# One row a lane of a projection weight loaded by GpSimd in four transfers, in a decode attention block

## The chip, the cores and the metric

The kernel runs on one core of a Trainium2 chip. The metric is device time in microseconds (us). A core has a matrix engine (PE), a vector engine (DVE), a scalar engine (ACT), GpSimd (POOL) and a sync engine (SP) that here only issues transfers. Sixteen DMA engines move data between the device memory and the on-chip memory, which has 128 lanes.

## The reference

One decode step of two blocks side by side on the same normalised input, added to it. `A` is attention with a cached K and V, `B` a gated MLP.

```python
x = A_x                                    # (4, 1, 640)
xn = _layernorm(x, axis=-1)
# A: 32 heads of 128, K and V caches of 4 x 32 x 4096 x 128, all bfloat16
q = (xn @ wq).reshape(B, Sq, Hq, Dh).transpose(0, 2, 1, 3)
scores = jnp.einsum('bhqd,bhkd->bhqk', q, k) * Dh ** (-0.5)
o = jnp.einsum('bhqk,bhkd->bhqd', _softmax(scores), v)
a = o.transpose(0, 2, 1, 3).reshape(B, Sq, Hq * Dh) @ wo      # wo: 4096 x 640
# B: w_in 640 x 1728, w_out 864 x 640
z = gelu(xn @ w_in); z1 = z[..., :864]; z2 = _layernorm(z[..., 864:])
g = einsum('ts,bsf->btf', w_sp, z2) + b_sp
return x + a + (z1 * g) @ w_out
```

Nearly all bytes are the two caches: 2 x 134 MB. The weights add 5.2 (wq), 5.2 (wo), 2.2 (w_in) and 1.1 MB (w_out).

## The kernel before, in words

The work is cut into 16 runs `i`, each one batch row and eight heads. A run's K is 128 lanes by 64 KB, as is its V. A large tile `ring` of 11 units (16 KB a lane each) holds whatever is in flight: wq first, then K of a run in four units, V in four, the weights of `B` for a while, and at the end `wo`.

**Loads.** Every large load is issued by SP, in the order of the list `loads` (lines 195 to 211): K of run 0 in halves, `w_in` and `w_out`, K and V in turn, and `load_wos` last. `pump()` (line 216) is called as units are given back and issues the next loads whose place is free, so SP is generally a transfer or two ahead of what is being moved. The last 96 rows of `w_out` come in six short transfers (`load_edge`, line 146), each 16 lanes of 1,280 B seen as 4 x 4.

**The projection weight.** `wo` is seen as four blocks `j` of 128 lanes by eight rows by 640 columns (line 168): a lane has eight rows of 1,280 B in a block, 10,240 B in one piece. `load_wo(j)` (line 172) loads blocks 0 to 2 by one transfer each and block 3 by three, cut at rows 5 and 7 (`WO_CUTS`). All six go out late, through `load_wos`, when the last V has its place.

**Compute.** For each quarter of K, DVE multiplies by q (`product`, line 542) and folds the halves (`fold`, line 551); PE adds up through an identity matrix (line 560), DVE finishes the row sums (line 573); then come the maximum, the exponential on ACT, and on PE the sums over V (`blocks`, line 635). At the end `group_proj` (line 747) multiplies each of the four head groups with its block of `wo`: eight rows `hh` by four column parts, 32 matmuls a block, in the order of the blocks. `res` is copied out of PSUM by ACT and DVE (lines 839 and 840), and SP and ACT store it.

**Order.** The lists of PE, DVE, ACT and SP inside `manual_schedule` are written out by hand. GpSimd's own list is short: some memsets, the identity, 16 small casts into `place` (line 294) that wait for `lane_diag` from DVE, and four small products late (line 695). A framework orders the instructions outside `manual_schedule` on each engine and inserts the waits. Near the start, `x` is normalised, transposed, and multiplied by wq (line 346); `stage_q` (line 516) spreads q over the lanes with `place`, and the result `qbc` is what `product` reads.

Of the kernel before, what the change touches and what calls it, by code (L numbers as in the profile page):

```python
# [10 lines left out]
BF16 = mybir.dt.bfloat16  # L11
# [9 lines left out]
def kernel(  # L21
# [14 lines left out]
    nc = tc.nc  # L36
    P = nc.NUM_PARTITIONS
    Bsz, Sq, D = A_x.shape
# [9 lines left out]
    HT = 8  # L48
# [24 lines left out]
    NOQ = D // CG  # L73
# [7 lines left out]
    const = ctx.enter_context(tc.tile_pool(name="const", bufs=1))  # L81
# [11 lines left out]
    def units(first, n=1):  # L93
        return ring[:, first * UNIT : (first + n) * UNIT]
# [73 lines left out]
    wo_r = A_wo.rearrange("(j p r) n -> j p (r n)", p=P, r=HT)  # L168
    wo_tiles = {}
    WO_CUTS = (0, 5 * D, 7 * D, HT * D)  # L170

    def load_wo(j):
        t = units(WO_UNIT, UNITS - WO_UNIT)[:, j * HT * D : (j + 1) * HT * D]
        wo_tiles[j] = t.rearrange("p (r n) -> p r n", r=HT)
        cuts = (0, HT * D) if j < HG - 1 else WO_CUTS
        for c0, c1 in zip(cuts, cuts[1:]):
            nc.sync.dma_start(out=t[:, c0:c1], in_=wo_r[j][:, c0:c1])

    def load_wos():
        for j in range(HG):  # L180
            load_wo(j)
# [34 lines left out]
    def pump():  # L216
        while loads:
# [21 lines left out]
        out=lane_diag[:],  # L239
        in_=ident_f[:].rearrange("p (h l) -> p l h", h=HT),  # L240
# [5 lines left out]
        out=hmask[:],  # L246
        in_=ident_f[:].rearrange("p (h l) -> p h l", h=HT),
# [5 lines left out]
        out=head_scale[:].rearrange("p (h l) -> p h l", h=HT),  # L253
# [11 lines left out]
        out=sel[:],  # L265
        in_=ident_f[:].rearrange("p (g h k) -> p k h g", g=CG, k=GC),
# [5 lines left out]
        out=spread[:],  # L272
        in_=ident[:].rearrange("p (m r) -> p r m", r=HT)[:, :, None, :].to_broadcast(
            [P, HT, HT, LN]
        ),
# [3 lines left out]
        out=q_lanes[:].rearrange("r b (h l) -> r b h l", h=HT),  # L279
        in_=ident[: HT * Bsz, : HT * Bsz]  # L280
# [9 lines left out]
    for g in range(CG):  # L290
        ps = slice(g * QW, (g + 1) * QW)
        for hh in range(QH):
            at_col = (g % 2 * QH + hh) * Bsz
            nc.gpsimd.tensor_copy(
                out=place[ps, hh, at_col : at_col + Bsz], in_=lane_diag[ps, 0:Bsz]
            )

    hmask_bf = const.tile([P, HT], BF16)
    nc.vector.tensor_copy(out=hmask_bf[:], in_=hmask[:])
# [8 lines left out]
    for i in range(NSTAT):  # L308
# [5 lines left out]
        out=rstd[:], in_=mv[:, 1:2], func=ACT.Sqrt, bias=eps_tile[:Bsz], scale=1.0  # L314
# [4 lines left out]
        out=xn_bf[:],  # L319
# [9 lines left out]
    for c in range(DC):  # L329
        nc.tensor.transpose(  # L330
            out=xnT_ps[:, c, :], in_=xn_v[:, c, :], identity=ident[:Bsz, :Bsz]
# [11 lines left out]
    for c in range(DC):  # L343
        for hg in range(NQG):
            g = hg % CG
            nc.tensor.matmul(
                out=q_ps[hg // CG][g * QW : (g + 1) * QW, :],
                lhsT=xnT[:, c, :],
                rhs=wq_sb[:, c, hg * QH * Dh : (hg + 1) * QH * Dh],
# [9 lines left out]
    def out_sum(half):  # L359
        return out_ps[OG * half : OG * half + Bsz, :]  # L360

    for half in range(2):
        nc.tensor.matmul(
            out=out_sum(half),
            lhsT=ident[:Bsz, :Bsz],
            rhs=x_bf[:, half * NOH : (half + 1) * NOH],
# [299 lines left out]
    def out_last(part):  # L666
        half, c = divmod(part, 2)
        at = OG * (2 * c + half)
        return finals[c][at : at + Bsz, 0:NOQ]
# [77 lines left out]
    def group_proj(hg):  # L747
        for hh in range(HT):
            for part in range(CG):
                nc.tensor.matmul(  # L750
                    out=out_last(part),
                    lhsT=gr[hg][:, hh, :],
                    rhs=wo_tiles[hg][:, hh, part * NOQ : (part + 1) * NOQ],
                    start=False,
                    stop=(hg == HG - 1 and hh == HT - 1),
                )

    E = mybir.EngineType
    with tc.manual_schedule(engines={E.PE, E.DVE, E.Activation, E.SP}):
# [73 lines left out]
        for hg in range(HG):  # L833
            group_proj(hg)
# [38 lines left out]
```

## Time and profile before

| | |
|---|---|
| median of 3 runs | 661.55 us (661.41 to 661.88) |
| the profiled execution | 661.42 us, span 659.3 us |
| bytes read | 282.24 MB, 428 GB/s over the span |
| DVE busy | 492.7 us (75%) |
| PE busy | 316.0 us (48%), granted clock 0.67 |
| ACT busy | 86.1 us (13%) |
| POOL busy | 8.5 us (1%), 31 instructions |

The profiled execution is one run with its own time; the span lies between its first and last instruction. In the views, a group of instructions stands under its line in the kernel, its engine and `tile written<-tile read`. The chain of waits goes back from the last instruction through whatever released it. A landing is the moment at which a DMA engine reports that its part of a transfer has arrived.

### The profile page before, as it was taken

Reading aid. Unit: us, or ns where it says so; the run is one execution under the profiler, and the core shown is the slowest. Engines: PE = TensorE matmul, PEld = TensorE weight load, DVE = VectorE, ACT = ScalarE, POOL = GpSimd, SP = SyncE. Lnnn points to the kernel's source line nnn. Section 1 sums busy time; section 2 is a strip of 40 time slices with the busy share of each in tenths; the row PEclk is TensorE's granted clock in tenths of the full one; section 3 lists DMA queues with packets and bytes.
Section 4 is the critical chain, followed back from the end, with each engine's and each line's share of the span. In section 5 each row is a group of like instructions: output and inputs, shape, how many; then the busy total and the mean of one; then the engine's idle time right before and its main releaser. Section 6 shows DMA issues by size and latency. Waiting matters only on the chain.

```text
span 659.3 us, 4830 instructions
## 1 busy us (share of the span) xinstructions
PE 316.0 (48%) x2063; PEld 144.2 (22%) x2063; DVE 492.7 (75%) x286; ACT 86.1 (13%) x208; POOL 8.5 (1%) x31
## 2 busy tenths in 40 slices
PE   0257552807446272644627165362715537245855
PEld 0114220302213130221303022130312213112323
DVE  2497968959496795949779494986949498699830
ACT  0023110020202002020210202002020200202000
POOL 3000000000000000000000000000000000000000
PEclk9676685755868566586856658685666868556776
DMA  9999999999999999999999999999999999999997
GB/s 380 433 449 418 432 441 437 426 446 437 422 437 418 441 442 425 441 430 421 441 445 430 441 418 430 441 434 433 438 421 437 431 429 438 445 425 422 426 429 301
DMA packets 6649, 282.56 MB, mean 429 GB/s; under 512 B 760, under 2 KB 996, under 8 KB 1380
## 3 DMA queue, kind: packets, MB, share of 16 engines
q1 hardware_dynamic: 6608, 282.24, 99.1%
q8 instruction: 16, 0.26, 0.1%
q14 instruction: 5, 0.04, 0.0%
q10 hardware_dynamic: 20, 0.01, 0.0%
HBM read 282.24 MB, written 0.01 MB: 428 GB/s over the span
## 4 chain that ended last, share of the span: by engine, by line
DMA 68%; DVE 21%; PE 10%; issue 1%; ACT 0%; SPq 0%; DVEq 0%
DMA ring<-in_A_k_cache_dram 60%; DVE ring L542 13%; PE s_ps L560 9%; DVE ring L551 7%; DMA ring<-in_A_wo_dram 4%; DMA ring<-in_A_v_cache_dram 4%; PE zT L405 1%; DVE s_sb L573 0%; PE s_ps L750 0%; PE max_ps L586 0%; PE ac_ps L483 0%; DVE m L582 0%; SPq L112 0%; DVE res L840 0%; ACT lay L584 0%
## 5 line engine op out<-in xcount | busy, mean ns | idle before, releaser
L542 DVE TENSOR_TENSOR ring<-ring,qbc 128x8192 bf16<-128x8192 bf16 x64 | 282.7, 4417 | 78.5 <-DMA ring<-in_A_k_cache_dram 78.5
L560 PE MATMUL s_ps<-ring,ident 128*128 128x512 bf16 x512 | 188.7, 535 | 248.0 <-DVE ring L551 248.0
L551 DVE TENSOR_TENSOR ring<-ring 128x4096 bf16<-128x4096 bf16 x64 | 146.6, 2291 | 2.0
L560 PEld LDWEIGHTS <-ident 128*128 128x128 bf16 x512 | 64.3, 129 | 356.3 <-issue 259.2
L635 PE MATMUL pv_acc<-ring,pm 128*32 128x512 bf16 x1024 | 83.7, 482 | 31.4 <-DMA ring<-in_A_v_cache_dram 31.4
L573 DVE TENSOR_REDUCE s_sb<-s_ps 128x64 f32<-128x512 f32 x64 | 43.8, 684 | 29.9 <-PE s_ps L560 29.9
L635 PEld LDWEIGHTS <-pm 128*32 128x32 bf16 x1024 | 44.6, 148 | 66.3 <-issue 57.9
L648 ACT COPY pv_sb<-pv_acc 128x512 f32<-128x512 f32 x16 | 9.4, 586 | 327.8 <-PE pv_acc L635 327.8
L607 ACT ACTIVATE pm<-p,hmask 128x256 bf16<-128x256 bf16 x120 | 49.5, 494 | 0.5
L652 PE MATMUL pv<-sel,pv_sb 128*128 128x8 f32 x128 | 16.9, 259 | 11.2 <-ACT pv_sb L648 11.2
L586 PE MATMUL max_ps<-lay,head_scale 128*128 128x16 f32 x32 | 7.0, 294 | 26.4 <-ACT lay L584 26.4
L652 PEld LDWEIGHTS pv<-sel,pv_sb 128*128 128x128 f32 x128 | 15.5, 191 | 18.5 <-ACT pv_sb L648 18.5
L584 ACT ACTIVATE lay<-lane_diag,m 128x16 f32<-128x16 f32 x16 | 4.9, 307 | 111.0 <-DVE m L582 111.0
L586 PEld LDWEIGHTS max_ps<-lay,head_scale 128*128 128x128 f32 x32 | 5.4, 211 | 36.1 <-ACT lay L584 36.1
L712 DVE TENSOR_TENSOR o_n<-pv,rden 128x32 bf16<-128x32 f32 x4 | 0.8, 191 | 15.0 <-PE pv L652 14.9
L592 DVE TENSOR_REDUCE nb<-max_ps 128x1 f32<-128x16 f32 x16 | 2.8, 173 | 11.8 <-PE max_ps L586 11.8
L695 POOL TENSOR_TENSOR own_sum<-acc,hmask 128x32 f32<-128x32 f32 x4 | 2.0, 500 | 612.5 <-ACT p L596 612.5
L596 ACT ACTIVATE p<-s_sb,nb 128x256 bf16<-128x256 f32 x16 | 8.1, 507 | 12.0 <-DVE nb L592 12.0
L528 ACT CAST q_rows<-qr_ps 32x128 bf16<-32x128 f32 x4 | 1.0, 256 | 58.9 <-PE qr_ps L520 58.9
L582 DVE TENSOR_REDUCE m<-s_sb 128x1 f32<-128x256 f32 x16 | 6.7, 420 | 0.5
L330 PE MATMUL xnT_ps<-ident,xn_bf 4*128 4x4 bf16 x5 | 0.4, 178 | 11.6 <-DVE xn_bf L318 11.6
L750 PE MATMUL s_ps<-ring,o_r 128*4 128x160 bf16 x128 | 4.5, 306 | 2.3 <-DMA ring<-in_A_wo_dram 2.3
(94 smaller groups left out, 79.1 us busy)
## 6 DMA issues: line engine op xcount, KB each, us to landing
ring<-in_A_v_cache_dram SPq DMA_DIRECT2D x6, 4096.0 KB, 18.4
ring<-in_A_k_cache_dram SPq DMA_DIRECT2D x2, 4096.0 KB, 33.8
ring<-in_A_wq_dram SPq DMA_DIRECT2D x1, 5120.0 KB
ring<-in_A_wo_dram SPq DMA_DIRECT2D x3, 1280.0 KB
ring<-in_B_w_in_dram SPq DMA_DIRECT2D x1, 2160.0 KB
ring<-in_B_w_out_dram SPq DMA_DIRECT2D x1, 960.0 KB
ring<-in_A_wo_dram SPq DMA_DIRECT2D x1, 800.0 KB
ring<-in_A_wo_dram SPq DMA_DIRECT2D x1, 320.0 KB
```

Of the source, the lines that this page charges most:

```text
L405: nc.tensor.matmul(out=zT[: P if k < NFF else TN, t, k, :], lhsT=w_t[:, 2 * c + t, k, :] if k < NFF else w_edge[:, 2 * c + t, k - NFF, :], ...
L542: nc.vector.tensor_tensor(out=t, in0=t, in1=qbcs[i // Bsz][:, i % Bsz, None, :].to_broadcast([P, QC, Dh]), op=ALU.mult,)
L551: nc.vector.tensor_tensor(out=t[:, :, 0:HD2], in0=t[:, :, 0:HD2], in1=t[:, :, HD2:Dh], op=ALU.add)
L560: nc.tensor.matmul(out=s[:], lhsT=ident[:], rhs=t[:, :, g * RW : (g + 1) * RW], start=(g == 0), stop=(g == n - 1),)
L573: nc.vector.tensor_reduce(out=scores[i][:, q * QC : (q + 1) * QC], in_=sums_ps.pop((i, q))[:], axis=AX.X, op=ALU.add,)
L582: nc.vector.tensor_reduce(out=m1[:], in_=scores[i][:], axis=AX.X, op=ALU.max)
L586: nc.tensor.matmul(out=ps[:], lhsT=head_scale[:], rhs=d[:], start=True, stop=True)
L596: nc.scalar.activation(out=p[:], in_=scores.pop(i)[:], func=ACT.Exp, bias=nb[:], scale=scale_qk, accum_out=acc[hg % NACC][:, b : b + 1],)
L607: nc.scalar.activation(out=p_m[i % 2][:, :, h, :], in_=probs[i][:].rearrange("p (n c) -> p n c", c=BC), func=ACT.Copy, scale=hmask[:, h : ...
L635: nc.tensor.matmul(out=pv_acc[g * CW : (g + 1) * CW, :], lhsT=pm[:, b0 // BC, :, :].rearrange("p h (k c) -> p c (h k)", k=GC)[:, c, :], rh ...
L648: nc.scalar.copy(out=pv_sb[:], in_=pv_acc[:])
L652: nc.tensor.matmul(out=pvs[hg][:, :, b], lhsT=pv_sb[:, k * Dh : (k + 1) * Dh], rhs=sel[:, k, :], start=(k == 0), stop=(k == GC - 1),)
```

## The change

Row 7 of block 0 of `wo`, one row of 1,280 B in each of the 128 lanes, gets a tile of its own, `wo_row`. GpSimd loads it in four transfers, of lanes 0 to 3, 4 to 61, 62 to 69 and 70 to 127. They stand in the program after the casts into `place`, and wait for nothing. SP's transfer of block 0 covers rows 0 to 6 only, 8,960 B of a lane's 10,240 in the device memory. `wo_tiles[j]` becomes a list of eight row views, of which the last one of block 0 is `wo_row`; `group_proj` reads the row from there.

```diff
     WO_CUTS = (0, 5 * D, 7 * D, HT * D)
+    ROW_CUTS = (0, 4, 62, 70, P)
 
     def load_wo(j):
         t = units(WO_UNIT, UNITS - WO_UNIT)[:, j * HT * D : (j + 1) * HT * D]
-        wo_tiles[j] = t.rearrange("p (r n) -> p r n", r=HT)
+        rows = t.rearrange("p (r n) -> p r n", r=HT)
+        wo_tiles[j] = [rows[:, r, :] for r in range(HT)]
         cuts = (0, HT * D) if j < HG - 1 else WO_CUTS
+        if j == 0:
+            wo_tiles[j][HT - 1] = wo_row
+            cuts = (0, (HT - 1) * D)
         for c0, c1 in zip(cuts, cuts[1:]):
             nc.sync.dma_start(out=t[:, c0:c1], in_=wo_r[j][:, c0:c1])
...
+    wo_row = const.tile([P, D], BF16, name="wo_row")[:]
+    for p0, p1 in zip(ROW_CUTS, ROW_CUTS[1:]):
+        nc.gpsimd.dma_start(out=wo_row[p0:p1], in_=wo_r[0][p0:p1, (HT - 1) * D :])
+
     hmask_bf = const.tile([P, HT], BF16)
...
                     lhsT=gr[hg][:, hh, :],
-                    rhs=wo_tiles[hg][:, hh, part * NOQ : (part + 1) * NOQ],
+                    rhs=wo_tiles[hg][hh][:, part * NOQ : (part + 1) * NOQ],
```

## The prediction

> **What bounds the kernel now.** I read the page's slices and queue table first, then the chain that ended last, then busy time by stage, then the chain's last 30 us, and below these the trace's DMA records (start, duration, bytes and queue of every packet, and the landings of every transfer).
>
> ```profile
> DMA  9999999999999999999999999999999999999997
> q1 hardware_dynamic: 6608, 282.24, 99.1%
> DMA 68%; DVE 21%; PE 10%; issue 1%; ACT 0%; SPq 0%; DVEq 0%
> ```
>
> The DMA engines are busy in every slice, and one queue, SP's, keeps all sixteen at 99.1%.
>
> ```profile
> 16.50:73.50 57.00, 29.40 (x202) 13.71 (x195) 44.12 (x37) 12.60 (x26) 0.00 (x0) 0.64 1.00 432
> 73.50:566.00 492.50, 234.37 (x1424) 105.62 (x1423) 379.62 (x192) 64.17 (x161) 0.72 (x3) 0.67 1.00 434
> 625.00:655.00 30.00, 17.18 (x233) 10.62 (x232) 6.53 (x13) 2.08 (x5) 1.28 (x1) 0.69 0.98 416
> ```
>
> The last columns are clock, DMA share and GB/s. The share is 1.00 from 16.5 to 566 us: the 21% that the chain gives to DVE is work during which DMA runs on, because SP issues the next transfer before the queue is empty (the smallest remainder I find is 4.7 us, when the second half of the first V block is issued at 65.96 and its forerunner lands from 70.69). Only the sum of the bytes counts, and at the end they are the limit alone:
>
> ```profile
> 626.10 28.87 DMA ring<-in_A_wo_dram
> 654.97 0.04 issue
> 655.02 1.56 PE s_ps L750 x26
> 656.58 0.02 issue
> 656.60 0.33 DVE res L840
> ```
>
> 654.97 is the landing of the last block's first cut. The two smaller cuts land at 655.76 and 656.18, each just as PE is through with the rows before it. So the last landing, 656.18, sets the end.
>
> That landing is sixteen landings, one a DMA engine: 653.26, 653.36, 653.84, 654.19, 654.41, 654.62, 654.71, 655.52, 655.83, 655.92, 656.06, 656.06, 656.07, 656.08, 656.17, 656.18. The slowest decides; the mean is 655.14, so perfect sharing of the same bytes would gain 1.04 us. The packet records show why they differ. Packets of one engine follow each other 4 ns overlapped and always at one rate (65,536 B in 2,418 ns), so sixteen chains can be followed by their phases. Sixteen packets of 16,384 B on queue 8 (instruction fetch, 885 to 962 ns) each push one chain back by about 1.41 us, for the next packet there is stretched too (2,886 to 2,967 ns). They go round eight engines: the ninth hits the chain of the first, and so on. Seven of those eight have had two by the tail and land from 655.83 on; the eighth has its second fetch after its last bytes. The six short transfers of line 151 (4 landings each) put 24 rows of 1,280 B on the same four engines, 24 x 52 ns = 1.25 us, and one of these four, with two 8,192 B packets of queue 14 besides, lands at 656.06. The four engines with neither are the first four landings.
>
> **The change part by part.** *Row 7 leaves SP's queue.* Block 0 goes from 128 packets of 10,240 B to 128 of 8,960 B. A 10,240 B packet has a pitch of 381 ns, a 1,280 B packet one of 52 ns (55 long), so 1,280 B more or less in a packet is 329 / 7 = 47 ns. Eight rows an engine: -0.38 us on every engine, at the tail. SP issues as many transfers as before:
>
> ```profile
> L177 SPq DMA_DIRECT2D ring<-in_A_wo_dram x6: 328/426/433, 614.1 to 626.9; - x6
> L151 SPq DMA_DIRECT2D ring<-in_B_w_out_dram x6: 630/636/795, 3.6 to 40.6; - x6
> ```
>
> *The row comes back on GpSimd's queue*, early. The same 163,840 B move earlier, which by itself is worth nothing: all sixteen engines are busy throughout. What counts is which engine gets how many of the 128 lanes. No row shows a GpSimd transfer. What is shown: transfers over 128 lanes land 16 times, those with an outer size of 4 land 4 times, single elements use one engine. [...] Twelve engines then get 1 lane (+0.05 us) and four get 29 (+1.51 us at 52 ns). [...]
>
> I take the value in which the 29 lanes fall on the four early engines. The late ones change by -0.38 + 0.05 = -0.33, so 656.18 becomes 655.85. The early ones change by -0.38 + 1.51 = +1.13 to 654.39, 654.49, 654.97 and 655.32, under 655.85. The gain is 0.33 us.
>
> *Price of a lane.* The row's lower end is 52 ns, that of SP's own 1,280 B packets. The upper end is the fetch, the farthest row: 1.41 us against 0.60 us for its bytes at the bulk rate, so 0.8 us more for one change of queue, times 29, some 23 us. I take 52 ns: the 2 B and 4 B packets of ACT's queue between the 40,960 B packets of SP's left the latter at 1,514 ns, the next starting 6 ns after. The margin is thin: the latest of the early four, 653.81 without the row, allows 2.04 / 29 = 70 ns for the full gain, 82 ns for none, and is 0.2% late at 127 ns.
>
> *GpSimd's four issues.* No row has their price. SP's issues above take 0.33 to 0.80 us, so 1.3 to 3.2 us for four; lower than nothing is excluded, as they replace nothing on GpSimd.
>
> ```profile
> 3.25 1.29 POOL L390 MEMSET ring<- 128x1440 bf16 x1
> 13.06 2.67 POOL L294 CAST place<-lane_diag 32x4 bf16<-32x4 f32 x16 [8.52 <-DVE lane_diag L238]
> 19.68 0.09 PEld L520 LDWEIGHTS <-place 64*32 64x32 bf16 x1 [0.42 <-issue]
> 21.47 0.59 ACT L535 CAST qbc<-qbc_ps 128x512 bf16<-128x512 f32 x1 [0.47 <-PE qbc_ps L531]
> 25.83 4.42 DVE L542 TENSOR_TENSOR ring<-ring,qbc 128x8192 bf16<-128x8192 bf16 x1 [5.55 <-DMA ring<-in_A_k_cache_dram]
> ```
>
> The transfers wait for nothing. Ahead of the casts of line 294 they fit in the 8.5 us for which GpSimd waits there, with xnT's memset (line 336) behind them, which DVE reads only at 13.98; behind the casts GpSimd is idle until 174.75. Late casts would first cost the 3.9 us between 15.73 and 19.68 and then the 3.8 us between 22.06 and 25.83. An issue would have to take over 4 us to be seen. Cost: nothing.
>
> *Earlier bytes.* By the first product a heavy engine has sent eight packets of wq and eight of K; with one row between any two that is 16 x 52 ns = 0.8 us, and the K landing of 25.73 can slip by so much. DVE's work for the first block slips too; the 4.7 us of queued bytes hide it. With that cover gone it would cost its 0.8 us.
>
> *PE* reads the last row of block 0 from another tile, after up to four more waits. Its first 64 matmuls of line 750 run from 649.66 to 651.46 and the next begins at 653.10: 1.6 us of idle time hide them.
>
> Sum: -0.33 us on the profiled execution's 661.42 (span 659.3 and 2.1 around it) is 661.09. The median shown is 661.55, 0.13 above that execution, so 661.2.
>
> **The rivals.** *Even spread:* each engine gets 8 to 10 lanes, at -0.38 + 0.42 to 0.52, so 0 to +0.14 us: 661.6. The 16 landings of 128-lane transfers speak for it, the 4 landings of the short ones against it. [...]
>
> *Heavy pairs on late engines:* the same spread, turned, puts 29 lanes on an engine ending at 656.06 to 656.18. That gives 656.18 + 1.13 = 657.31, 1.13 us slower: 662.7. Nothing in the trace tells where GpSimd's first transfer starts.
>
> *Every short transfer starts at the same engine* (the slower side): line 151's six did so. Then two of its four engines, which end between 654.41 and 656.06, get 1 + 29 + 1 + 29 = 60 lanes, 3.12 - 0.38 = +2.74 us: 657.15 to 658.80, 1.0 to 2.6 us slower, 663.3 in the middle. On the latest of the four it takes the gain from 10 lanes (656.18 less 655.68, over 52 ns) and passes 0.2% at 35.
>
> *A dear lane:* at 150 ns the four early engines end at up to 653.81 + 4.35 = 658.16, 2.0 us slower, 663.5; it hurts from 82 ns.
>
> **How the numbers follow.** Forecast 0.50, even spread 0.14, pairs on late engines 0.12, same start 0.09, dear lane 0.10, and 0.05 for a gain of over 0.2%: perfect sharing gives 1.04 us, so it needs fewer or cheaper fetches too. 0.2% is 1.3 us, about what a measurement of this kernel can tell from no change. Slower by over that are most of same start (0.06) and dear lane (0.09) and a third of the late pairs (0.05), with 0.01 for the rest: 0.21. Faster by over that is the last case, 0.05. Within it: 0.74. The range goes from 660.6 (perfect sharing, rounded) to 663.0, past the late pairs and part of the last two. The forecast's own range is 660.9 to 661.5.
>
> **What would show it.** Right: 1,280 B packets on a new queue, 29 in each of four chains and 1 in each of twelve; 8,960 B packets of about 338 ns; the last landing 0.3 us earlier and the sixteen landings within some 1.5 us rather than 2.9; GpSimd's issues over before 13 us or after 15.7, and the first product within 0.8 us of 25.83. Wrong: a chain with 58 rows or more, a heavy chain among those with fetches, rows more than 70 ns apart or stretched packets beside them, or fetches that go to other engines than now.

## The result, and the profile after

| | before | changed |
|---|---|---|
| median of 15 runs each | 661.58 us (661.41 to 661.88) | 662.64 us (662.41 to 664.81) |
| ratio to before | | 1.0018, 95% interval 1.001 to 1.0026 |
| profiled execution | 661.42 us, span 659.3 us | 662.85 us, span 660.7 us |

The kernel became slower by 0.18% (interval 0.10 to 0.26%), about 1.1 us, where a gain of 0.3 us was forecast.

From the profile of the changed kernel: the DMA share by slices, the queues that moved the weights and caches, and the chain that ended last, by engine.

```profile
DMA  9999999999999999999999999999999999999996
q1 hardware_dynamic: 6608, 282.08, 99.0%
q0 software_dynamic: 128, 0.16, 0.1%
DMA 72%; DVE 19%; PE 9%; issue 1%; SPq 0%; DVEq 0%
```

The new queue q0 is GpSimd's, with 0.16 MB in 128 packets. SP's queue lost as much and fills the DMA engines as before. Nothing at this level tells of a loss. The end of the chain does tell that it is the DMA that is late:

```profile
627.85 28.53 DMA ring<-in_A_wo_dram
656.38 0.04 issue
656.42 1.50 PE s_ps L759 x30
657.92 0.02 issue
657.95 0.33 DVE res L849
```

The landing that starts the last 32 matmuls came at 654.97 and now comes at 656.38, 1.41 us later, as much as the span grew. The other end of the run shows where the time was lost. These are six rows of GpSimd, PE and DVE around the start, in order of time:

```profile
2.99 1.72 POOL L305 DMA_DIRECT2D wo_row<-in_A_wo_dram  x3
12.99 2.77 POOL L299 CAST place<-lane_diag 32x4 bf16<-32x4 f32 x16 [8.28 <-DVE lane_diag L243]
15.70 0.54 POOL L305 DMA_DIRECT2D wo_row<-in_A_wo_dram  x1
16.27 0.23 POOL L345 MEMSET xnT<- 128x160 bf16 x1
17.07 4.28 PE L355 MATMUL q_ps<-ring,xnT 128*32 128x512 bf16 x40 [4.85 <-DMA ring<-in_A_wq_dram]
27.17 4.42 DVE L551 TENSOR_TENSOR ring<-ring,qbc 128x8192 bf16<-128x8192 bf16 x1 [5.32 <-DMA ring<-in_A_k_cache_dram]
```

The first product starts at 27.17 rather than 25.83, 1.34 us later, and waits for its K, not for GpSimd: three issues took 1.72 us, the fourth 0.54. So the loss is made within 27 us, and the rest of the run, in which the DMA engines never rest, hands it on.

The packet records show how. Between 7 and 26 us, SP's packets of one size took one time before, within 7 ns; in the changed kernel nearly half of them took longer (a packet is counted as longer from 4 ns on):

```
SP's packets that start between 7 and 26 us     before          changed
40,960 B, normally 1,514 ns                     0 of 79 longer  49 of 78 longer, by up to 384 ns
32,768 B, normally 1,213 ns                     2 of 159        50 of 136, by up to 405 ns
time added, per DMA engine                      0.00 us         1.06 us
GpSimd's own packets, per DMA engine            -               0.48 us
SP's packets of block 0 at the tail             385 ns each     338 ns each: -0.38 us per engine
```

The sum, 1.06 + 0.48 - 0.38 = 1.16 us, is the loss of the mean engine: from SP's first packet to the mean of the last sixteen landings it was 653.40 us and is 654.56, 1.16 us more. The last of the sixteen went from 656.18 to 657.52, and their spread stayed (2.91 and 2.86 us), so no single engine carries the loss. The course fits too: counted from each kernel's first packet, SP's packets are on average 1.52 to 1.57 us later than before from 22 us on, which is 1.06 + 0.48, and about 1.17 us later once block 0 has gone by. The stretched packets lie where the two transfers of 58 lanes move: they start at 9.7 to 13.2 and 18.8 to 21.7 us. The 4 lanes at 7.0 to 8.6 us stretch nothing; beside the 8 lanes, at 13.9 to 15.5 us, packets are longer by some 20 to 90 ns.

And the lanes are dealt otherwise than forecast. Each transfer of 58 lanes is 14 packets of 5,120 B (four lanes), one of 2,568 B (two lanes and 8 B) and one of 16 B, one packet on each of the sixteen engines: four lanes on fourteen, two on one, none on the last. No engine has 29.

### The profile page after: what moved, and what is told of

It reads as the page before. It is cut to its first block, busy times and chain, and to the rows that moved or that the text cites. A ratio compares the mean times of both kernels' runs of the same rounds, so it can differ in the third digit from the quotient of the medians.

```text
span 660.7 us, 4837 instructions
## 1 busy us (share of the span) xinstructions
PE 312.0 (47%) x2063; PEld 143.2 (22%) x2063; DVE 492.9 (75%) x286; ACT 86.1 (13%) x208; POOL 10.8 (2%) x35
## 4 chain that ended last, share of the span: by engine, by line
DMA 72%; DVE 19%; PE 9%; issue 1%; SPq 0%; DVEq 0%
DMA ring<-in_A_k_cache_dram 64%; DVE ring L551 12%; PE s_ps L569 8%; DVE ring L560 6%; DMA ring<-in_A_wo_dram 4%; DMA ring<-in_A_v_cache_dram 4%; PE s_ps L759 0%; DVE s_sb L582 0%; SPq L112 0%; DVE res L849 0%; PE den L711 0%; DVEq L551 0%
## 5 line engine op out<-in xcount | busy, mean ns | idle before, releaser
L569 PE MATMUL s_ps<-ring,ident 128*128 128x512 bf16 x512 | 186.2, 529 | 251.5 <-DVE ring L560 251.5
L661 PEld LDWEIGHTS pv<-sel,pv_sb 128*128 128x128 f32 x128 | 15.5, 191 | 18.8 <-ACT pv_sb L657 18.8
L721 DVE TENSOR_TENSOR o_n<-pv,rden 128x32 bf16<-128x32 f32 x4 | 0.8, 192 | 15.5 <-PE pv L661 15.4
L355 PE MATMUL q_ps<-ring,xnT 128*32 128x512 bf16 x40 | 4.3, 614 | 4.9 <-DMA ring<-in_A_wq_dram 4.9
```

What stands on the lines that cost most here:

```text
L569: nc.tensor.matmul(out=s[:], lhsT=ident[:], rhs=t[:, :, g * RW : (g + 1) * RW], start=(g == 0), stop=(g == n - 1),)
L661: nc.tensor.matmul(out=pvs[hg][:, :, b], lhsT=pv_sb[:, k * Dh : (k + 1) * Dh], rhs=sel[:, k, :], start=(k == 0), stop=(k == GC - 1),)
```

## The experiments

Two theories were set up for the stretch. The *lanes theory* is a supposition, as no trace shows which lanes an engine writes: in every transfer over 128 lanes an engine would write the same eight (block 0 is 128 packets for sixteen engines); a transfer over fewer lanes would deal them anew from its first lane on (packets of 5,120 B, four lanes to an engine, in the transfers of 58 lanes), so that an engine writes lanes of another; then both would be held up, and those behind them. The *queue theory*: packets of GpSimd's queue hold up SP's packets on the same engine, whatever their lanes.

**One transfer of 128 lanes.**

```diff
-    ROW_CUTS = (0, 4, 62, 70, P)
+    ROW_CUTS = (0, P)
```

> The row goes on GpSimd's queue in one transfer of 128 lanes in place of four. Lanes theory (a DMA engine that writes lanes which another engine's large transfers write holds both up): with 128 lanes each engine writes the lanes that it always writes, so SP's packets are not stretched beside it (under 0.1 us an engine, against 1.0 us with the four); 0.4 to 0.5 us for the row's own packets early, 0.31 us back at the tail, so 0.1 to 0.2 us slower than before, 661.7 us. Queue theory (packets of GpSimd's queue hold up SP's on the same engine, whatever their lanes): the same bytes on the same queue, so the stretch stays near 1.0 us and the time near that of the four transfers, 662.6 us.

Measured: 661.61 us (661.50 to 661.73) beside 661.55 before, ratio 1.0 (0.9991 to 1.0009). From its page, the line of GpSimd's queue, and then from its chain the start of the last block's matmuls:

```profile
q0 software_dynamic: 48, 0.16, 0.1%
```

```profile
655.06 0.04 issue
655.10 1.51 PE s_ps L759 x29
```

The same 0.16 MB on the same queue, and PE starts the last block at 655.10, against 655.02 before and 656.42 in the changed kernel. Of SP's packets between 7 and 26 us, 4 are longer, 0.01 us an engine; the row's own packets are 32 of 5,120 B, 0.40 us an engine, and 0.40 - 0.38 = 0.02 us is what the row costs. The queue theory falls for GpSimd's queue as such.

**Two transfers of 64 lanes.**

```diff
-    ROW_CUTS = (0, 4, 62, 70, P)
+    ROW_CUTS = (0, P // 2, P)
```

> The row goes on GpSimd's queue in two transfers of 64 lanes. Lanes theory: all sixteen engines write four lanes each inside one half of the lanes, so eight of them write lanes of others; SP's packets are stretched about as much as with the four transfers, 0.8 to 1.3 us an engine, and the time is 662.4 to 662.9 us. Queue theory: no difference to the one transfer of 128 lanes, within 0.2 us.

Measured: 662.58 us (662.31 to 662.95), ratio 1.0015 (1.0006 to 1.0024). The same place of its chain:

```profile
656.11 0.04 issue
656.16 1.51 PE s_ps L759 x32
```

There are again 32 packets of 5,120 B, two on each engine as with the one transfer; what differs is, by the lanes theory, the lanes that each engine writes, and there are 16 more packets of 4 B. 67 of 80 packets of 40,960 B between 7 and 26 us are stretched, by up to 425 ns, 0.84 us an engine, and PE's last block starts 1.06 us later than with one transfer.

**Two halves on SP's queue, late.** GpSimd loads nothing.

```diff
-    for p0, p1 in zip(ROW_CUTS, ROW_CUTS[1:]):
-        nc.gpsimd.dma_start(out=wo_row[p0:p1], in_=wo_r[0][p0:p1, (HT - 1) * D :])
...
-    ROW_CUTS = (0, 4, 62, 70, P)
+    ROW_CUTS = (0, P // 2, P)
...
             cuts = (0, (HT - 1) * D)
+            for p0, p1 in zip(ROW_CUTS, ROW_CUTS[1:]):
+                nc.sync.dma_start(out=wo_row[p0:p1], in_=wo_r[0][p0:p1, (HT - 1) * D :])
```

> No transfer on GpSimd's queue: SP loads the row in two halves of 64 lanes just before the seven other rows of block 0, so all bytes stay on SP's queue and in their old place. Lanes theory: the stretch appears here too, 0.5 to 1.2 us an engine in the packets beside the halves at about 640 us, and the time is 0.5 to 1.2 us over before, 662.1 to 662.8 us. Queue theory: no stretch, 661.6 us, the time of before within 0.2 us.

Measured: 662.68 us (662.50 to 662.91), ratio 1.0016 (1.0007 to 1.0025). The first two lines of its queues on the page:

```profile
q1 hardware_dynamic: 6768, 282.24, 99.1%
q8 instruction: 16, 0.26, 0.1%
```

There is no q0, all bytes are on SP's queue and in their old place, and the loss is that of the changed kernel. Between 7 and 26 us no packet is longer by over 5 ns; between 628 and 650 us, 179 of 595 packets are longer, 0.80 us an engine (before: one, beside an instruction fetch, 0.03). Neither GpSimd's queue nor the early place is needed.

**The four transfers, without using the row.** PE reads block 0 as before.

```diff
-        if j == 0:
-            wo_tiles[j][HT - 1] = wo_row
-            cuts = (0, (HT - 1) * D)
```

> The four transfers of GpSimd are made, but the row is not used: SP loads block 0 in full as before and PE reads it from there. Both theories: this is the cost of the four transfers alone, 0.48 us of own packets and 1.0 us of stretch an engine, so 1.5 us over before, 663.1 us, and 0.3 us over the changed kernel, whose shorter packets of block 0 give that back. Were the stretch caused by the 8,960 B packets or by the new reader of the row instead, the time would be 0.5 us over before at most, 662.1 us.

Measured: median of six runs 663.8 us (662.85 to 664.99), ratio 1.0033 (1.0022 to 1.0045). The six are three at 662.85 to 663.08 and three at 664.5 to 665.0; the profiled one, 662.85, is of the first group, 1.4 us over the profiled execution before, where 1.5 was expected. Its stretch is 0.76 us an engine, smaller than the changed kernel's 1.06 for the same transfers, so this cost varies by some 0.3 us between executions. What the upper group is stays open, as no profile shows one; one of the fifteen executions of the changed kernel, 664.81, lies there too. The run shows that the loads alone cost all of the loss, not the tail's part.

**Another source.** The kernel with one transfer on GpSimd's queue, but reading rows that lie 64 lanes further on.

```diff
+    wo_q = A_wo.rearrange("(q r) n -> q (r n)", r=HT)
...
-        nc.gpsimd.dma_start(out=wo_row[p0:p1], in_=wo_r[0][p0:p1, (HT - 1) * D :])
+        nc.gpsimd.dma_start(out=wo_row[p0:p1], in_=wo_q[64 + p0 : 64 + p1, (HT - 1) * D :])
```

> As the one transfer of 128 lanes on GpSimd's queue, but each lane is filled from the row that lies 64 lanes further on in the device memory, so that the engines read rows other than those they always read and write the lanes they always write (row 7 of block 0 gets a wrong row for it). Lanes theory: it is the written lanes that count; SP's packets are not stretched (under 0.1 us an engine after the first 7 us) and the time is that of the one transfer, 661.6 us within 0.2. Source theory (what counts is which rows of the device memory an engine reads): stretch as with the halves, 0.8 us an engine, 662.5 us.

Measured: 661.72 us (661.53 to 662.10), ratio 1.0001 (0.9992 to 1.001); one of 229 packets is longer, by 15 ns. In the runs so far an engine that wrote other lanes, by the lanes theory, also read other rows; here, by the same theory, it reads other rows and writes its own lanes, and the median is 0.14 us over before. Other rows alone stretch nothing, so what counts is the side that is written.

**The same shape, on lanes 0 to 63 and on lanes 64 to 127.** To the kernel before, an extra load is added ahead of block 0 that nobody reads, 64 lanes as two transfers of 8 by 4, that is eight shares of four lanes; each transfer lands eight times, so on eight engines. The twin differs in the rows read and the lanes written alone.

```diff
+        if j == 0:
+            for p0 in (0, 32):          # the twin: (64, 96)
+                src = wo_r[0][p0 : p0 + 32, (HT - 1) * D :]
+                nc.sync.dma_start(
+                    out=wo_row[p0 : p0 + 32], in_=src.rearrange("(k e) n -> e k n", e=8)
+                )
```

> The kernel before, with an extra load late on SP's queue that nobody reads: lanes 0 to 63 of the row in two transfers of 8 by 4 lanes, so that eight engines write eight lanes each. Lanes theory: these are lanes that the same eight engines write in the large transfers; the cost is 8 x 52 ns = 0.4 us on eight engines and no stretch, 0.2 to 0.5 us over before, 661.8 to 662.1 us. Rival (transfers over less than 128 lanes hold up the others whatever their lanes): stretch of 0.3 us and more an engine, 0.8 to 1.2 us over before, the same as its twin on lanes 64 to 127.

> The twin of the last run: the same two extra transfers of 8 by 4 lanes at the same place, into lanes 64 to 127. Lanes theory: the same eight engines now write lanes that the other eight write in the large transfers; the packets beside them are stretched on all sixteen, and the time is 0.5 to 1.0 us over its twin's, 1.0 to 1.4 us over before, 662.5 to 663.0 us. Rival (short transfers whatever their lanes): the time of its twin within 0.2 us.

Measured: 662.12 us (661.95 to 662.53), ratio 1.0007 (0.9998 to 1.0016), on lanes 0 to 63; 662.79 us (662.64 to 663.16), ratio 1.0018 (1.0009 to 1.0027), on lanes 64 to 127. The chains' ends, first of the one, then of the twin:

```profile
655.41 0.04 issue
655.45 1.57 PE s_ps L758 x30
```

```profile
656.30 0.04 issue
656.34 1.53 PE s_ps L758 x31
```

The same number of packets, of the same sizes, on the same queue at the same time, and 0.9 us between them (0.67 us between the medians). The packet records of 628 to 650 us:

```
                       SP's packets longer   time added, per engine   the 64 packets of 1,280 B
lanes 0 to 63          1 of 559              0.03 us                  55 ns each
lanes 64 to 127        112 of 524            0.77 us                  55 to 91 ns
```

This is the clearest pair. On lanes 0 to 63, the eight engines carry their rows and disturb nobody, for 0.54 us, a little over the upper end expected; on lanes 64 to 127 as many bytes add 0.77 us to the mean engine. The 0.67 us between the medians lie within the expected 0.5 to 1.0 us. The pair alone leaves a rival: short transfers into the upper 64 lanes might hold up the others whoever writes them. The changed kernel excludes it, as its first transfer of 58 lanes goes to lanes 4 to 61 only and stretches sixteen packets in a row by 202 to 384 ns.

**The tail's part alone.** The eighth row of block 0 is not loaded at all.

```diff
-    for p0, p1 in zip(ROW_CUTS, ROW_CUTS[1:]):
-        nc.gpsimd.dma_start(out=wo_row[p0:p1], in_=wo_r[0][p0:p1, (HT - 1) * D :])
+    nc.gpsimd.memset(wo_row, 0.0)
```

> The tail's part of the change alone: SP loads seven rows of block 0, and the eighth is never loaded but zeros from a memset of GpSimd (so 163,840 B less are read and the row's share of the sum is missing). Both theories: 8 x 47 ns = 0.38 us of packets less on every engine (0.31 us as measured in the changed kernel), nothing early: 0.3 to 0.4 us faster than before, 661.2 us. Were the seven rows or PE's reading from another tile a cost of their own, it would be less.

Measured: 661.26 us (661.08 to 661.66) beside 661.58, a difference of 0.32 us as expected, though the ratio's interval, 0.9987 to 1.0005, holds 1. Five of the eleven executions, the profiled one (661.62) among them, are at 661.40 to 661.66, hardly faster or not at all. In the profiled one the mean of the last sixteen landings, from the first packet on, is 0.34 us earlier than before, but the last of them stands at 656.28, against 656.18. The 128 packets of 338 ns are in the trace, eight an engine and 47 ns shorter than before; that is 0.38 us, not the 0.31 us that two of the expectations give for it. So 0.38 us an engine is the most that taking the row off the tail can give, and every engine has to carry it again elsewhere.

## Why the prediction was wrong

*What bounds the kernel* held: the time of the DMA engines decides (SP's queue at 99.0%), and a loss made within 27 us stood undiminished until the tail, where block 0 gave 0.38 us back. So did the tail's term: -0.38 us by 338 in place of 385 ns; the run that left the row out shows it in the mean landing (-0.34 us) and, within the noise, in the median (-0.32 us).

*Where the lanes go* failed. The sum's terms of 29 lanes on four engines and 1 lane on each of the twelve others, +1.51 and +0.05 us, are shown by no run; in the changed kernel each transfer of 58 lanes put four lanes on fourteen engines, two on one and none on the last. The SP transfers seen before (16 landings over 128 lanes, 4 over an outer size of 4) said nothing of how GpSimd's 58 lanes would be dealt. With the deal that came, the prediction's *even spread* was the right rival, and its sum was 0 to +0.14 us. It fell short too: the split cost 1.0 us, and in one transfer the row was free (661.61 us).

*The price of a lane* is the step that made the sign wrong. Its 52 ns hold: GpSimd's own packets come to 0.42 us an engine, 0.48 with those of 4 and 16 B. What is missing in the sum, in the forecast and in the even spread alike, is what a row costs the others: +1.06 us on the mean engine, from stretched packets of SP, a term that stood at nothing. The prediction did name stretched packets as a sign of being wrong. The rows that the price rested on could not show it. Beside SP's short transfers of line 151 (to lanes 0 to 15 and 32 to 47; 41.30 to 42.87 and 61.69 to 62.40 us before) all 74 of its larger packets took their usual 291, 1,213 or 2,418 ns, and among its transfers over 128 lanes 2 of 238 packets were longer, by up to 7 ns. The extra load over lanes 0 to 63 left 558 of 559 as they were, and beside GpSimd's row over 128 lanes 4 were longer, 0.01 us an engine. The far upper bound, the instruction fetch, was a price of changing queues, and no queue is to blame: the halves on SP's queue cost as much.

The lanes theory fits all these runs but is not shown by them: the traces have a packet's time and size, not the lanes it writes. The twin runs fit it if their eight engines are those that write lanes 0 to 63 in the large transfers: 0.03 us added on lanes 0 to 63, 0.77 on 64 to 127. What was measured is that the written lanes (this pair, with the other source at no cost) and the deal of them (0.01 us an engine in one transfer of 128 lanes, 0.84 in two of 64) decide, not through which part.

*The rivals.* The late pairs came nearest in time, 662.7, by a cause that is not there: no engine had 29 lanes. The same start and the dear lane did not occur; a lane was not dear to its own engine (0.48 us of GpSimd's packets) but to SP's packets (1.06 us).

*GpSimd's issues* cost nothing, as forecast, at 0.51 to 0.68 us each, but their place was not one of the two foreseen: the fourth stands behind the casts and pushes xnT's memset behind itself, from 2.99 to 16.27 us. DVE's copy of xnT moved from 13.98 to 16.54, and q's matmuls start at 17.07, released by wq. That q is spread by 23.6 us (ACT's cast starts at 23.04) and K lands at 27.1 leaves 3.5 us of cover. *The earlier bytes* were allowed 0.8 us at the first product and took 1.34.

The range, 660.6 to 663.0, holds 662.64, but by luck: its upper part stood for heavy pairs on late engines. The forecast of no change within 0.2% was right in size and wrong in direction: the interval, 1.001 to 1.0026, excludes 1.

## What to carry to other kernels

When DMA engines are the bound, a transfer over a part of the lanes can cost more than its own bytes: here 80 to 160 KB in such transfers stretched the other packets by 0.8 to 1.1 us on the mean engine. The same row over all 128 lanes in one transfer added 0.01 us to them, so try that first. If a transfer has to be partial, measure more than one choice of lanes: 8 by 4 over lanes 0 to 63 added 0.03 us, the same over 64 to 127 0.77. To judge such an edit, compare the durations of equal packets beside it: here they were constant within a few nanoseconds until something held them up.

## What the runs showed of the hardware that was not expected

- A DMA engine's packets of one size mostly take one time (before, 3,548 of 3,584 of 65,536 B in 2,418 ns and, from 7 us on, 40,960 B in 1,514 to 1,516), and in the changed kernel the sixteen that start between 9.71 and 10.79 us, beside the first transfer of 58 lanes, are all stretched, by up to 384 ns. Even engines that have no packet of that transfer in flight yet are hit: the first stretched packets, by 202 to 206 ns from 9.71 us on, are of engines whose own packet of the transfer follows only at their end, 1.7 us on.
- One transfer of 128 lanes from GpSimd's queue beside SP's full queue cost SP's packets 0.01 us an engine: here two queues on one engine cost each other nothing.
